# An attention kernel followed by two MoE layers: gammas' product on GpSimd, twelve constant products ahead of the first q and k, and the first MoE's weight conversions placed beside attention pairs

## The chip, the cores and the metric

One Trainium2 chip, one core. A NeuronCore has TensorE (matmuls, into PSUM), VectorE, ScalarE, GpSimd and SyncE, which run separate in-order instruction queues, and 16 DMA engines. In the profile they are PE (with PEld for its weight loads), DVE, ACT, POOL and SP; in this kernel SP's queue issues nearly all DMAs. The metric is the device time in microseconds of one execution; lower is better.

## The reference

```python
def attn(q, k, v, g_q, g_k):          # batch 4, heads 12, seq 448, head_dim 64
    q_n, k_n = rmsnorm(q, g_q), rmsnorm(k, g_k)
    scores = q_n @ k_n.T / sqrt(64)
    p = softmax(scores)               # max subtracted, sum + 1e-9
    return p @ v                      # v is 0.1 * randn

def moe(x, w_in, w_out, g_ln):        # 1792 tokens, 768 -> 1024 -> 768
    h = x @ w_in
    solu = h * softmax(h)
    ln = (solu - mean) / sqrt(var + 1e-6) * g_ln
    return ln @ w_out

def moe2(x, w_in, w_out):             # 768 -> 2048 -> 768
    h = x @ w_in
    return (h - tanh(h)) @ w_out

out = moe2(moe(attn(...) as 1792 tokens x 768, ...), ...)
```

The weights of both MoE layers arrive as float64, so their DRAM tensors are read as pairs of int32.

## The kernel before

**Attention.** The 48 heads are worked on as 24 pairs p. `load_qk` (L209) loads q and k of a pair, `norm` (L241) computes the reciprocal root mean squares (square on ScalarE, reduction and the rest on VectorE) and scales, `qk_trans` (L264) transposes on TensorE, splits each value into a high and a low float32r part, multiplies k by `gam` (the product of both gammas and the scale, one [128, 1] column) and for p > 0 spreads the parts by DMA into the layouts `Q` and `K`. `maxima` (L325) gets each row's maximum from one matmul and a VectorE reduction; `spread` (L345) transposes the maxima and puts them by a small DMA (`q<-nt`) into a row of `Q`, so that the scores of `weights` (L357) come out with the maximum subtracted; ScalarE takes the exponential. `pv` (L391) multiplies by v, `pv_fin` and `x_norm` divide by the sum, and x_norm stores the pair's result into the DRAM tensor `xd` (L432), which tells in the trace when a pair is done.

**First MoE.** Tokens are worked on in four blocks of 384, 384, 384 and 640. `x_split` (L490) loads a block of xd, `moe_h` (L500) is the first product, `layer_norm` (L539) the activation, `moe_lnT` (L571) transposes and `moe_x2` (L585) is the second product. `stage(b)` (L602) does x_split(b), moe_lnT(b-1), moe_h(b), layer_norm(b) and moe_x2(b-1).

**Weights.** `Stream` (L96) brings weight tiles in: `fetch` (L111) loads 512 KB of raw int32 pairs by SP's queue into the pool `raw_p` (two buffers), and `convert` (L117) makes a high and a low float32r part of it (512 KB together). A converted tile that is needed in later blocks too is saved to DRAM (L164) and loaded again from there (L174). There are twelve input tiles ("in") and twelve output tiles ("out", multiplied by the layer norm's gamma on the way). For a saved tile the conversion is: ScalarE's absolute value (L135), VectorE's maximum (L136), shift (L140) and two merges (L144, L147); then for an input tile ScalarE's copy (L160) and GpSimd's subtraction (L161), for an output tile four ScalarE copies (L154) and four VectorE operations (L155). `conv(n)` (L167) brings the stream up to item n and looks two items ahead with its loads. In the kernel before, input tiles come by conv in `moe_h(0)`, and the twelve output tiles are converted in `moe_h(1)` (L534 to 536), three after each quarter of the input weights, in the pool Bp["w"] of five buffers that also holds the reloaded input tiles.

**Order.** The list `attn` holds every attention step with a slot and a step in it (`at`, L438): slot 2p begins pair p's maxima, its norm is at slot 2p - 3, its last step at slot 2p + 3. `attn_next` runs the next (slot, step). The program first runs all steps up to slot 15 (L679), then `overlap(b, batch)` (L682) spreads the remaining ones over stages 0, 1 and 2 (slots 16 to 27, 28 to 39, 40 and up). The written order isn't the queues' order: the tile framework plans with a simulated timeline, so that an instruction whose operands and buffers are there early in the plan may be queued ahead of earlier-written ones. So the raw loads and conversions of the first input tiles, written in stage 0, stand in the queues among the first attention pairs. After attention, the second MoE (`h2`, `out2`, from L786 on) runs in eight rounds over its own weight stream.

The start: identity and constants are built, the two gammas are loaded by ScalarE's DMA queue (L676) and multiplied on VectorE (L678):

```python
nc.vector.scalar_tensor_tensor(out=gam, in0=gam, scalar=scale, in1=gam2, op0=ALU.mult, op1=ALU.mult)
while attn_left(H + 3):
    attn_next()
```

## Time and profile before

| | |
|---|---|
| median of 3 runs | 1116.38 us (1116.32 to 1119.02) |
| profiled execution, its own time | 1117.29 us |
| its span on the core | 1115.4 us |
| PE busy | 1045.5 us, 94% |
| DVE busy | 694.8 us, 62% |
| ACT busy | 493.8 us, 44% |
| POOL busy | 234.2 us, 21% |
| moved by DMA | 171.20 MB |

Busy times are those of the one profiled execution; matmuls are pipelined, so a busy PE isn't one at its peak. A row of a timeline gives the start, the duration, the engine, the line of the kernel, the operation with output and inputs, how many of them, and in brackets how long the engine was idle before and what ended that. DMA share is the mean busy share of the 16 DMA engines; the clock column is the TensorE clock that the throttle granted, as a fraction.

### The profile page before, as it was taken

What the parts mean: (1) busy time and instruction counts of PE and PEld (TensorE: products, weight loads), DVE (VectorE), ACT (ScalarE), POOL (GpSimd) and SP (SyncE); (2) the same over time, 40 slices, a digit from 0 to 9 for tenths busy, and PEclk for the clock granted to TensorE, in tenths of its full rate; (3) what the DMA queues carried; (4) which work ended last, traced back from release to release, by engine and by line L of the source; (5) the groups of instructions that cost most, each with busy time, mean ns of one, the idle gap of its engine ahead of it and who ended that gap; (6) DMA issues with size and microseconds to landing.
All of it is one profiled execution on the core that took longest, in us unless ns stands there. A gap on an engine that the chain in (4) does not pass through costs nothing.

```text
span 1115.4 us, 15528 instructions
## 1 busy us (share of the span) xinstructions
PE 1045.5 (94%) x5528; PEld 874.9 (78%) x5528; DVE 694.8 (62%) x1313; ACT 493.8 (44%) x1004; POOL 234.2 (21%) x204
## 2 busy tenths in 40 slices
PE   4989999988987899998999999999999999999998
PEld 2555666657774778777899989898999989898987
DVE  8776687788797353724655057375767666675444
ACT  4677777777676454744246154321212121212110
POOL 2411123131102000001500025242314241322000
PEclk9999999999998999998999999999999999999999
DMA  7987779957997978655767443121111111120004
GB/s 184 258 230 192 184 213 282 229 167 209 288 285 231 307 207 260 182 174 174 249 205 242 156 152 92 34 65 49 57 38 57 58 58 57 57 57 1 1 29 170
DMA packets 108945, 171.20 MB, mean 153 GB/s; under 512 B 31748, under 2 KB 73156, under 8 KB 108868
## 3 DMA queue, kind: packets, MB, share of 16 engines
q1 hardware_dynamic: 107568, 170.20, 52.2%
q8 instruction: 44, 0.72, 0.3%
q14 instruction: 33, 0.27, 0.1%
q10 hardware_dynamic: 1300, 0.01, 0.1%
HBM read 109.32 MB, written 29.10 MB: 124 GB/s over the span
## 4 chain that ended last, share of the span: by engine, by line
PE 74%; DMA 12%; DVE 7%; ACT 5%; issue 2%; SPq 1%; POOL 0%; ACTq 0%; DVEq 0%; POOLq 0%
PE pvps L401 8%; PE ops L183 7%; PE ops L184 7%; PE ops L182 7%; PE h2ps L183 7%; PE h2ps L184 7%; PE h2ps L182 7%; PE sps L378 4%; PE x2ps L182 3%; PE x2ps L183 3%; PE x2ps L184 3%; PE hps L182 2%; PE hps L184 2%; DMA xr<-xd 2%; PE hps L183 2%; DMA q<-wq 2%
## 5 line engine op out<-in xcount | busy, mean ns | idle before, releaser
L780 DVE TENSOR_TENSOR ob<-ops,ob 128x384 f32<-128x384 f32 x196 | 108.6, 555 | 103.0 <-PE ops L184 102.4
L161 POOL TENSOR_TENSOR w<-val,w 128x512 fp32r<-128x512 f32 x60 | 81.3, 1356 | 419.7 <-ACT w L160 402.6
L401 PE MATMUL pvps<-pf,va 128*128 128x448 f32 (+1 forms) x384 | 160.9, 583 | 1.7 <-ACT pf L387 1.7
L183 PE MATMUL ops<-w,gT 128*128 128x384 f32 x448 | 150.7, 336 | 0.0
L182 PE MATMUL ops<-w,gT 128*128 128x384 f32 x448 | 150.6, 336 | 0.0
L184 PE MATMUL ops<-w,gT 128*128 128x384 f32 x448 | 150.5, 336 | 0.0
L343 DVE TENSOR_REDUCE nm<-mps 128x1 f32<-128x448 f32 x168 | 102.9, 620 | 66.3 <-PE mps L342 57.6
L183 PE MATMUL h2ps<-x2s,w 128*128 128x512 f32 (+1 forms) x384 | 141.0, 367 | 0.0
L184 PE MATMUL h2ps<-x2s,w 128*128 128x512 f32 (+1 forms) x384 | 140.9, 367 | 0.0
L182 PE MATMUL h2ps<-x2s,w 128*128 128x512 f32 (+1 forms) x384 | 140.6, 367 | 0.0
L378 PE MATMUL sps<-q,k 128*128 128x448 f32 (+1 forms) x368 | 117.5, 413 | 20.7 <-ACT pf L387 9.2
L757 ACT ACTIVATE th<-h2ps 128x512 f32<-128x512 f32 (+1 forms) x64 | 34.8, 544 | 181.2 <-PE h2ps L184 180.9
L378 PEld LDWEIGHTS sps<-q,k 128*128 128x128 f32 (+1 forms) x368 | 63.0, 186 | 55.5 <-ACT pf L387 17.8
L387 ACT ACTIVATE pf<-sps 128x448 f32<-128x448 f32 x167 | 88.3, 539 | 37.9 <-PE sps L378 29.5
L182 PE MATMUL hps<-w,xs 128*128 128x256 f32 x336 | 101.0, 301 | 2.7 <-DMA w<-w_in 2.5
L184 PE MATMUL hps<-w,xs 128*128 128x256 f32 x336 | 96.5, 288 | 0.0
L183 PE MATMUL hps<-w,xs 128*128 128x256 f32 x336 | 95.6, 285 | 0.0
L401 PEld LDWEIGHTS pvps<-pf,va 128*128 128x128 f32 (+1 forms) x384 | 61.6, 195 | 42.1 <-issue 34.3
L342 PE MATMUL mps<-k,q 128*128 128x448 f32 (+1 forms) x144 | 77.2, 545 | 14.9 <-DVE nm L343 5.6
L258 POOL TENSOR_TENSOR qn<-qk,rr 112x512 f32<-112x512 f32 x44 | 47.5, 1101 | 192.5 <-DVE rr L239 88.9
L183 PEld LDWEIGHTS ops<-w,gT 128*128 128x128 f32 x448 | 84.3, 188 | 4.6
L182 PEld LDWEIGHTS ops<-w,gT 128*128 128x128 f32 x448 | 84.2, 188 | 4.6 <-DVE ob L780 0.2
(117 smaller groups left out, 2091.7 us busy)
## 6 DMA issues: line engine op xcount, KB each, us to landing
w<-w_out SPq DMA_DIRECT2D x48, 512.0 KB
raw<-in_moe_w_in_dram SPq DMA_DIRECT2D x36, 512.0 KB
raw<-in_moe_w_out_dram SPq DMA_DIRECT2D x36, 512.0 KB
w<-w_in SPq DMA_DIRECT2D x36, 512.0 KB
k<-wk SPq DMA_DIRECT2D x46, 224.0 KB
q<-wq SPq DMA_DIRECT2D x46, 224.0 KB
w_in<-w SPq DMA_DIRECT2D x12, 512.0 KB
w_out<-w SPq DMA_DIRECT2D x12, 512.0 KB
```

What stands on the lines that cost most here:

```text
L161: nc.gpsimd.tensor_tensor(out=w[:, 1], in0=x, in1=w[:, 0].bitcast(F32), op=ALU.subtract)
L182: nc.tensor.matmul(ps, lhsT=a[0], rhs=w[0], start=first, stop=False)
L183: nc.tensor.matmul(ps, lhsT=a[0], rhs=w[1], start=False, stop=False)
L184: nc.tensor.matmul(ps, lhsT=a[1], rhs=w[0], start=False, stop=last)
L258: eng.tensor_tensor(out=qn[:, a].rearrange("p c h d -> p h c d"), in0=t[:, a], in1=rr[:, a].rearrange("p h (c o) -> p h c o", o=1).to_broa ...
L342: nc.tensor.matmul(ps, lhsT=qh[:, f:f + 128], rhs=kh, start=True, stop=True)
L343: nc.vector.tensor_reduce(out=nm_t[p][:, c:c + 1], in_=ps, axis=AX.X, op=ALU.max, negate=True)
L378: nc.tensor.matmul(o, lhsT=K[p % NQ][:, i, z, k0:k0 + m], rhs=qcols(Q[p % NQ], slice(0, 128), p, i, z), start=(z == 0), stop=(z == 1))
L387: nc.scalar.activation(out=x, in_=ps, func=AF.Exp)
L401: nc.tensor.matmul(pv_t[n], lhsT=w, rhs=pc_t.pop((n, j))[r], start=first, stop=last)
L757: nc.scalar.activation(out=th, in_=ps, func=AF.Tanh)
L780: nc.vector.tensor_tensor(out=o, in0=ps, in1=o, op=ALU.add)
```

## The change

Four edits. The product of the gammas moves to GpSimd, as two instructions. Twelve matmuls of the identity with itself, into a PSUM tile that nobody reads, are issued after the first load. The input tiles 0 to 4 of the first MoE are converted at attention slots 3, 5, 7, 9 and 11, each raw load written directly ahead of its conversion, with no look ahead. The twelve output tiles are no longer converted in moe_h(1): `conv_out` fetches and converts them at slots 4, 6, 8, 10, 12 and 13 to 19, in a new pool "wp" with one raw buffer and one result buffer. Up to the end of the steps before stage 0, raw loads are pinned: they stand on SP's queue behind all DMAs written ahead of them.

```diff
+    pinned = [True]
...
-        def fetch(self, kind, i):
+        def fetch(self, kind, i, pool=None):
             if (kind, i) not in self.raw:
                 src, (a, b) = source(kind, i)
-                t = self.raw[kind, i] = raw_p.tile([128, a, b, 2], I32, tag="raw", name="raw64")
-                nc.sync.dma_start(out=t, in_=src)
+                t = self.raw[kind, i] = (pool or raw_p).tile([128, a, b, 2], I32, tag="raw", name="raw64")
+                dma = nc.sync.dma_start(out=t, in_=src)
+                if pinned[0]:
+                    tc.keep_in_program_order(dma)
...
-        def conv(self, n):
+        def conv(self, n, ahead=2):
...
-                self.load(self.nc + 2)
+                self.load(self.nc + ahead)
...
+    def conv_out(i):
+        ws.fetch("out", i, A["wp"])
+        ws.convert("out", i, A["wp"], True)
+
...
+    for i in range(5):
+        at(3 + 2 * i, 3, lambda i: ws.conv(i + 1, 0), i)
+    for i in range(12):
+        at((4, 6, 8, 10, 12, 13, 14, 15, 16, 17, 18, 19)[i], 3, conv_out, i)
...
                         ws.conv(w0 + 3 * qq + 6)
-                        if b == 1:
-                            for i in range(3 * qq, 3 * qq + 3):
-                                ws.convert("out", i, Bp["w"], True)
...
-        ("pc", 6), ("xu", 1), ("xo", 1), ("small", 2),
+        ("pc", 6), ("wp", 1), ("xu", 1), ("xo", 1), ("small", 2),
...
     attn_next()
+
+    warm = ps_x.tile([128, 4, CP], F32, tag="x", name="warm")
+    for _ in range(12):
+        nc.tensor.matmul(warm.rearrange("p c q -> p (c q)")[:, 0:128], lhsT=idf, rhs=idf, start=True, stop=True)
...
-    nc.vector.scalar_tensor_tensor(out=gam, in0=gam, scalar=scale, in1=gam2, op0=ALU.mult, op1=ALU.mult)
+    nc.gpsimd.tensor_scalar(out=gam, in0=gam, scalar1=scale, scalar2=None, op0=ALU.mult)
+    nc.gpsimd.tensor_tensor(out=gam, in0=gam, in1=gam2, op=ALU.mult)
     while attn_left(H + 3):
         attn_next()
+    pinned[0] = False
```

## Rows read from the trace of the kernel before

**Rows 1.** The page's busy times: engine, busy us, share of the span, instructions.

```profile
PE 1045.5 (94%) x5528; PEld 874.9 (78%) x5528; DVE 694.8 (62%) x1313; ACT 493.8 (44%) x1004; POOL 234.2 (21%) x204
```

**Rows 2.** Windows: stretch, length, busy PE, PEld, DVE, ACT, POOL; clock, DMA share, GB/s.

```profile
15.00:60.60 45.60, 40.44 (x117) 22.42 (x117) 36.08 (x71) 27.57 (x59) 15.28 (x14) 1.00 0.94 253
60.60:142.20 81.60, 75.33 (x315) 47.04 (x315) 53.86 (x106) 60.59 (x131) 14.74 (x18) 0.98 0.76 194
...
142.20:237.40 95.20, 86.90 (x442) 61.25 (x440) 75.37 (x140) 69.33 (x147) 25.66 (x24) 0.98 0.89 238
237.40:394.60 157.20, 134.22 (x679) 102.02 (x680) 117.30 (x260) 103.06 (x234) 22.91 (x26) 0.96 0.85 256
394.60:508.00 113.40, 111.70 (x617) 89.86 (x616) 49.64 (x98) 63.05 (x130) 5.84 (x9) 1.00 0.71 205
280.00:320.00 40.00, 35.92 (x206) 28.14 (x204) 33.06 (x74) 29.85 (x75) 5.75 (x6) 0.96 1.02 293
```

**Rows 3.** Timeline of the start, all engines.

```profile
5.33 0.63 ACT L250 ACTIVATE sq<-qk 112x512 f32<-112x512 f32 x1 [1.10 <-DMA qk<-in_q_dram]
8.14 0.16 DVE L678 SCALAR_TENSOR_TENSOR gam<-gam,gam 128x1 f32<-128x1 f32 x1 [3.18 <-DMA gam<-in_g_k_dram]
8.21 1.27 DVE L252 TENSOR_REDUCE ss<-sq 112x8 f32<-112x512 f32 x2
...
11.01 0.98 PE L268 MATMUL qkps<-idf,qn 112*128 112x112 f32 x4 [11.01 <-DVE nr L238]
...
12.03 0.63 ACT L279 ACTIVATE k<-qkps,gam 128x448 fp32r<-128x448 f32 x1 [0.15 <-PE qkps L268]
```

**Rows 4.** Timeline of TensorE around 41 us, then windows as in Rows 2.

```profile
40.58 0.57 PE L373 MATMUL sps<-q,k 64*128 64x448 f32 x1
42.68 0.37 PE L373 MATMUL sps<-q,k 64*128 64x448 f32 x1
12.00:16.00 4.00, 2.25 (x9) 1.61 (x9) 3.95 (x15) 3.00 (x9) 0.00 (x0) 1.00 0.83 239
60.00:64.00 4.00, 1.62 (x7) 1.08 (x8) 2.46 (x4) 1.56 (x5) 0.00 (x0) 1.00 0.97 253
64.00:68.00 4.00, 4.00 (x14) 1.84 (x13) 2.97 (x8) 3.21 (x9) 0.00 (x0) 0.65 0.80 236
```

**Rows 5.** Timeline of SP's queue: raw weight loads and stored pairs.

```profile
10.68 0.65 SPq L115 DMA_DIRECT2D raw<-in_moe_w_in_dram  x1
...
60.59 0.58 SPq L432 DMA_DIRECT2D xd<-xo  x1
...
68.49 0.43 SPq L115 DMA_DIRECT2D raw<-in_moe_w_in_dram  x1
...
142.24 0.54 SPq L432 DMA_DIRECT2D xd<-xo  x1
...
179.71 0.40 SPq L115 DMA_DIRECT2D raw<-in_moe_w_out_dram  x1
```

**Rows 6.** Lines by form: conversions from 20 to 60 (first row), from 260 to 360.

```profile
L161 POOL TENSOR_TENSOR w<-val,w 128x512 fp32r<-128x512 f32 x5 | 7.1, 1427 | 23.0 <-DVE nr L237 17.1 <-ACT w L160 5.9
...
L154 ACT ACTIVATE w<-val,gln 128x128 fp32r<-128x128 f32 x48 | 15.3, 390 | 0.9 <-DVE val L147 0.8
L155 DVE SCALAR_TENSOR_TENSOR w<-val,gln,w 128x128 fp32r<-128x128 f32 x48 | 14.3, 348 | 0.5 <-DMA va<-in_v_dram 0.2 <-ACT w L154 0.2
L144 DVE SCALAR_TENSOR_TENSOR val<-raw,val 128x512 int32<-128x512 int32 x11 | 8.8, 797 | 0.2
L147 DVE SCALAR_TENSOR_TENSOR val<-raw,val 128x512 int32<-128x512 int32 x10 | 7.5, 749 | 0.1
L135 ACT ACTIVATE val<-raw 128x512 f32<-128x512 f32 x10 | 6.7, 669 | 8.1 <-DMA raw<-in_moe_w_out_dram 6.4 <-DVE nm L343 1.4
L140 DVE TENSOR_SCALAR val<-val 128x512 int32<-128x512 int32 x11 | 5.4, 488 | 0.1
```

**Rows 7.** Timeline of ScalarE: the longest early wait for a raw load.

```profile
28.78 0.67 ACT L135 ACTIVATE val<-raw 128x512 f32<-128x512 f32 x1 [2.37 <-DMA raw<-in_moe_w_in_dram]
```

**Rows 8.** GpSimd's one small operation, line L563: min/median/max ns.

```profile
L563 POOL TENSOR_TENSOR rs<-rs,mhalf x14: 544/560/2137, 229.6 to 592.5; 128x1 f32<-128x1 f32 x14
```

## The prediction, made before the changed kernel was run

> **What bounds the kernel now.** I read the busy times first, then the windows stage by stage, then the timeline of the start, then the SP queue. Over the whole span TensorE is busy 94% [rows 1], which says little: the 600 us after the attention, more than half of it, are not touched by the change. The stages ahead of them differ, and the windows [rows 2] show it. There the attention of four batches runs with the first MoE; I name the stretches *front* (15 to 60.6, until the first pair's result is stored), *prologue* (60.6 to 142.2, six further pairs, almost only attention), *stage 0* (to 237.4), *stage 1* (to 394.6) and *stage 2* (to 508). The reader is to compare the last two. Both do 384 tokens of the first MoE's two products beside about six pairs of attention; stage 1 issues 679 matmuls in 157.2 us, stage 2 617 in 113.4. Stage 2 is TensorE-bound (111.7 of 113.4 busy), while in stage 1 VectorE is busy 117.3 against 49.6, ScalarE 103.1 against 63.1, and the DMA share is 0.85 against 0.71. What stage 1 has and stage 2 has not is the conversion of the twelve tiles of output weights. The prologue has nearly no conversions and runs at 13.6 us a pair; the front has five complete ones of input weights [rows 6], nine raw loads being issued from 10.68 to 68.49 [rows 5], and a DMA share of 0.94.
>
> **The change part by part.**
>
> *Gammas' product on GpSimd.* VectorE sits 3.18 us for gamma's DMA at 8.14, with the first norm's reduction queued behind it; ScalarE's squares are over by 5.96 [rows 3]. Off that queue, the reduction starts about 5, then waits at most for ScalarE, and the first transposes move from 11.01 to about 8.0: 3.0 us. The product is first used at 12.03, so then at 9.0. It is now two instructions; the only small GpSimd instruction in the trace takes 560 ns [rows 8], so gamma is ready near 8.1 + 2 x 0.56 = 9.2, and the gain is 2.7. Behind it on GpSimd stand zero fills not needed for several us. Bounds 2 to 3.
>
> *Twelve constant products.* They need the identity only and fill TensorE from some 3 us to the first transposes, on an idle engine: nothing lost. What they can give is the clock. The granted-clock column says 1.00 from the start, but the durations do not: the same matmul takes 0.57 at 40.58 and 0.37 at 42.68 [rows 4], so TensorE works at 1.2 GHz until 41 us and at 2.4 from there. Later the clock falls once after a stretch with 1.62 of 4 us busy (granted 0.65 next) [rows 4]. From 12 to 16 TensorE is busy 2.25 of 4 at the low level, which is some 1.1 of 4 at the high one: thinner than the stretch after which it fell. So I think it likelier that the raised clock is lost again before the dense part. The Trainium skill, "TensorE: Matmul & The Clock Gate", Part 1, says that the default state is throttled, that activity releases it and that idleness takes it back; by its release alone the products would pay in full, by its second half they would not. The fall at 64 agrees with the second half, the rise at 41 with the first.
>
> *The front.* Its DMA work is 0.94 x 45.6 = 42.9 us. Seven of the nine raw loads and five saves lie in it; 512 KB at 293 GB/s per 1.02 share [rows 2] is 1.8 us each, so half of that work leaves. At the prologue's pace (81.6 us / 315 matmuls = 0.26) the front's 117 matmuls are 30.3 us, 15 less than now: with the 2.7 that is -18 if the clock is high from the beginning. If it is low until 41 as before, only the some 60 matmuls after that gain (19.6 to 15.6): -7. Without raw loads in the way TensorE becomes dense earlier and its clock should rise earlier; I take **-13**.
>
> *The prologue* pays. Input tiles 0 to 4 are converted at slots 3 to 11 and output tiles at slots 4 to 15, so 13 conversions with 13 raw loads and 13 saves lie in these 12 slots, which held two raw loads. DMA: 0.76 x 81.6 = 62.0, less 2 x 1.8, plus 13 x 3.4 (3.65 by the mixed rate above; the attention part of that mix moves at 194/0.76 = 255 GB/s by its own row, so the conversions' part is faster) = 102.6; at the 1.02 that 280 to 320 holds [rows 2] it is 100.6 us. VectorE: an output tile costs 4 x 0.348 + 0.797 + 0.749 + 2 x 0.488 = 3.9, an input tile 2.5 [rows 6]: 53.9 + 5 x 2.5 + 8 x 3.9 = 97.6. ScalarE: 0.67 + 4 x 0.39 = 2.2 and 1.3: 60.6 + 6.5 + 17.8 = 85. The DMA queues end last: 100.6 instead of 81.6, **+19**. Bounds: +5, if the conversions slide into later slots (their pool has one raw buffer and one result buffer, so one conversion must free the raw buffer before the next load, and nothing in the attention waits for them); +28, if ScalarE also waits for each raw load.
>
> *Stage 0* keeps its seven input tiles and gets four output tiles: 13.6 us of DMA, 15.6 of VectorE. It loses raw loads of output weights that were issued there early, the first at 179.71 [rows 5]. Its DMA work is 0.89 x 95.2 = 84.7, its VectorE 75.4: there is room for most. **+6**, bounds 0 and +13.
>
> *Stage 1* gives back. At stage 2's pace it takes 113.4 plus the 62 further matmuls at 134.22/679 = 0.20 each, 12.3: 125.7 instead of 157.2, **-32**. It also does norms and loads of six pairs where stage 2, at the end of attention, does fewer; so -20 to -35. What is late next in stage 1 is TensorE itself. Nothing waits for the saved output tiles there before its second product.
>
> *Order on the SP queue.* Pinned raw loads cost issue time in any place (some 0.4 each [rows 5]); moved behind the attention's loads they no longer delay those of the first pairs. The pin itself adds no wait: a pinned load may be issued later than written, not earlier. Each new load or save that stands at the head of SP and waits delays the small loads of maxima behind it; that is in the +28.
>
> Sum: -13 + 19 + 6 - 32 = **-20** on a span of 1115.4. The profiled execution took 1117.29, the median is 1116.38: **1096**.
>
> **The rivals.**
>
> *A, slack absorbs it.* The clock stays high (-18), conversions slide to where engines have room (+5, +3), stage 1 reaches stage 2's pace with less overhead (-35): -45, 1071. For: TensorE's peak demand in the prologue is below its span, and at 280 to 320 VectorE is busy 33.06 of 40 under a full DMA while TensorE still holds 35.92 [rows 2]. Against: DMA demand of prologue and stage 0 together (62 + 84.7 + 17 x 3.4 less the early raw loads, about 195) exceeds their 176.8 us.
>
> *B, the price is conserved.* The twelve output tiles cost 31.5 us in stage 1, 2.6 each. At that price prologue and stage 0 pay 31 for them, and the five input tiles take with them what they cost in the front: 0, within 3 us of 1116. The change would move the load, not hide it. The same time results if the planner's order lets the output tiles slide so far that stage 1 still holds them.
>
> *C, slower: ScalarE waits for the raw loads.* Now a raw load is issued long ahead; even so ScalarE waited 2.37 us at the head of its queue for one [rows 7]. After the change the load is issued just ahead of its conversion, and behind the waiting instruction on ScalarE stand the exponentials for which TensorE waits. 13 x 2.4 = 31 on top of 85 busy is 116, +35 in the prologue; four more in stage 0, +13; front only -10, stage 1 -28: +10, 1126. It decides from about 1.6 us a conversion upward, where ScalarE's 85 + 13 x 1.6 = 106 passes the DMA's 100.6 and adds to its jitter.
>
> **How the numbers follow.** Forecast 0.5, A 0.2, B 0.13, C 0.17. A measurement of this kernel can tell about 0.3% (3.3 us) from no change. The forecast's own bounds reach from 1077 to 1112, all on the faster side. Faster: 0.5 + 0.2 + a quarter of B = 0.73; same: 0.10; slower: C = 0.17. The range runs from 1071 (A) to 1115 (most of B); it leaves out C and the ends of A.
>
> **What would show it.** First transposes at 8.0 to 8.5; matmul durations of the first maxima at the low level again after some us; the first pair stored at 47 to 50 and the seventh at 142 to 150; a DMA share near 1.0 between them; no output conversion after the start of stage 1, and stage 1 at 122 to 137 us with VectorE below half. Wrong would be: a share well below 1 in the prologue with ScalarE waiting on raw loads (C), conversions in stage 1 (B), or a full clock through the front (A). The second MoE should only shift.

## The result, and the profile after

| | before | after |
|---|---|---|
| median | 1118.67 us (6 runs, 1116.32 to 1123.95) | 1135.36 us (6 runs, 1128.35 to 1141.29) |
| profiled execution, span | 1117.29, 1115.4 us | 1135.99, 1134.2 us |

The changed kernel is slower: ratio 1.0148, 95% interval 1.0101 to 1.0195. The forecast was 1096.0, range 1071 to 1115. (The lines of the code that the trace names have moved down by 4 to 14: L135 is now L139, L279 is L283, L342 is L346, L378 is L382.)

The busy times of the changed kernel's page answer to [rows 1]. TensorE is busy 15 us longer for the same work and 24 extra matmul records (the constant products, 4.5 us ahead of the first transposes); VectorE's, ScalarE's and the DMA's totals have not moved. So nothing else was added but time in which TensorE waits or runs slowly.

```profile
PE 1060.5 (94%) x5552; PEld 883.4 (78%) x5552; DVE 694.4 (61%) x1312; ACT 493.5 (44%) x1004; POOL 237.0 (21%) x206
```

The windows of the changed kernel, cut at the same events as [rows 2] (first and seventh pair stored, then the starts of stage 1 and stage 2); the columns are those of [rows 2]:

```profile
15.00:63.40 48.40, 45.07 (x116) 25.22 (x116) 25.57 (x52) 22.68 (x49) 9.78 (x10) 0.60 0.55 139
63.40:168.60 105.20, 85.88 (x339) 51.95 (x338) 79.74 (x170) 77.53 (x176) 22.47 (x22) 0.94 0.92 254
168.60:288.70 120.10, 96.99 (x436) 62.28 (x435) 106.23 (x212) 84.80 (x186) 32.91 (x30) 0.93 0.86 254
288.70:414.00 125.30, 121.72 (x671) 97.57 (x670) 69.43 (x143) 77.26 (x165) 17.25 (x21) 0.99 0.78 217
```

| stretch | before | after | difference | forecast |
|---|---|---|---|---|
| front, to the first pair's store | 45.6 (to 60.6) | 48.4 (to 63.4) | +2.8 | -13 (-7 to -18) |
| prologue | 81.6 | 105.2 | +23.6 | +19 (+5 to +28) |
| stage 0 | 95.2 | 120.1 | +24.9 | +6 (0 to +13) |
| stage 1 | 157.2 | 125.3 | -31.9 | -32 (-20 to -35) |
| rest of the span | | | -0.6 | 0 |

The sum is +18.8, the span's difference. Stage 1 gave back exactly what was forecast; the front gave nothing, and stage 0 cost four times its term. A part of the prologue's time is work taken ahead: it holds 339 matmul records against 315 before, 15 of the 24 more of the first MoE's first product.

**The start.** The timeline of the changed kernel answers to [rows 3]:

```profile
3.09 4.51 PE L676 MATMUL warm<-idf 128*128 128x128 f32 x24 [3.09 <-POOL idf masks.py:199]
7.93 0.19 POOL L693 TENSOR_TENSOR gam<-gam,gam 128x1 f32<-128x1 f32 x1 [1.02 <-DMA gam<-in_g_k_dram]
7.96 0.60 PE L272 MATMUL qkps<-idf,qn 112*128 112x112 f32 x4 [0.36 <-DVE qn L262]
15.86 1.06 ACT L254 ACTIVATE sq<-qk 112x1024 f32<-112x1024 f32 x1 [4.22 <-DMA qk<-in_q_dram]
16.83 0.62 ACT L283 ACTIVATE k<-qkps,gam 128x448 fp32r<-128x448 f32 x1
17.50 0.74 PE L338 MATMUL mps<-k,qd 128*128 128x448 f32 x1 [5.68 <-ACT k L283]
```

The first transposes start at 7.96 as forecast (8.0), at the high clock (0.60 instead of 0.98 for four). But k's copy on ScalarE, which is ready to run then, stands behind the square of pair 2 (L254), and that waits 4.22 us for its DMA. So the first maxima start at 17.50, while the kernel before has 15.44 and three us less would have been 12.4. TensorE has nothing from 11.8 to 17.5 and its clock falls. The windows of four us show that it stays down (PE busy, then the clock column):

```profile
12.00:16.00 4.00, 0.00 (x0) 0.00 (x0) 0.29 (x1) 0.14 (x1) 0.00 (x0) 0.65 0.88 225
28.00:32.00 4.00, 4.00 (x9) 1.99 (x7) 0.86 (x3) 0.54 (x1) 2.04 (x2) 0.50 0.99 246
48.00:52.00 4.00, 4.00 (x8) 1.64 (x7) 2.07 (x6) 0.85 (x3) 0.61 (x1) 0.50 0.01 3
52.00:56.00 4.00, 4.00 (x9) 1.55 (x7) 1.35 (x3) 2.01 (x4) 2.15 (x3) 0.73 0.28 59
```

**The prologue.** In all of it ScalarE waits 9.9 us in 5 for raw loads; the longest of these waits shows the chain. All engines of the changed kernel, timeline from 82 us, rows picked: a raw load of an output tile is issued at 82.74, ScalarE's absolute value (L139) stands at the head of its queue 4.39 us for it, VectorE's maximum (L140) waits 4.68 us for that, a reduction of maxima (L347) stands behind VectorE's conversion steps, and TensorE's next maxima matmul (L346) waits 3.36 us for the reduction.

```profile
82.74 0.44 SPq L117 DMA_DIRECT2D raw<-in_moe_w_out_dram  x1
...
88.17 1.22 ACT L139 ACTIVATE val<-raw 128x512 f32<-128x512 f32 x2 [4.39 <-DMA raw<-in_moe_w_out_dram]
88.86 0.43 DVE L140 TENSOR_SCALAR val<-val 128x512 f32<-128x512 f32 x1 [4.68 <-ACT val L139]
...
90.00 0.62 DVE L347 TENSOR_REDUCE nm<-mps 128x1 f32<-128x448 f32 x1
...
90.67 1.02 PE L346 MATMUL mps<-k,q 128*128 128x448 f32 x2 [3.36 <-DVE nm L347]
```

And the windows around it: ScalarE did nothing at all and VectorE 0.18 us from 84 to 88, TensorE 1.24 us of the next four; and then four us at 0.61 of the clock.

```profile
84.00:88.00 4.00, 3.32 (x15) 1.92 (x13) 0.18 (x1) 0.00 (x0) 1.91 (x3) 1.00 0.90 272
88.00:92.00 4.00, 1.24 (x3) 0.67 (x4) 3.10 (x7) 3.75 (x8) 0.00 (x0) 0.97 1.09 238
92.00:96.00 4.00, 3.89 (x13) 1.85 (x11) 4.00 (x8) 3.36 (x9) 0.00 (x0) 0.61 0.92 204
```

**Stage 0.** VectorE is busy 106.23 of 120.1 us here. The forecast had 75.4 + 15.6 = 91. The groups by line of this stretch (168.6 to 288.7) show what more there is: twelve conversions of saved tiles (L140) where the forecast had eleven, and two of tiles that aren't saved (L142), which belong to the second MoE. The lines of the conversions are 46.3 us of VectorE here against 21.1 before, so 25 of the 31 us that it has more. In the kernel before, those two have their raw loads at 343.96 and 355.17, in stage 1; in the changed kernel SP issues them from 248.96 on, two together: with the output tiles gone from stage 1 the raw buffers are free early.

```profile
L140 DVE TENSOR_SCALAR val<-val 128x512 f32<-128x512 f32 x12 | 5.7, 476 | 7.4 <-ACT val L139 7.4
...
L142 POOL TENSOR_SCALAR val<-raw 128x512 f32<-128x512 f32 x2 | 3.7, 1855 | 8.5 <-DMA raw<-in_moe_w_in_dram 8.5
```

They meet block 0's layer norm. Two of the windows of that stretch:

```profile
268.00:272.00 4.00, 1.64 (x3) 0.58 (x3) 4.00 (x9) 1.10 (x2) 0.00 (x0) 0.65 1.00 240
272.00:276.00 4.00, 1.85 (x3) 0.79 (x4) 4.00 (x9) 1.23 (x3) 0.00 (x0) 0.50 1.00 356
```

From 264 to 284 TensorE is busy 12.1 of 20 us (2.63 + 1.64 + 1.85 + 3.28 + 2.71 in the five windows), the last 12 of them at half clock, and its waits from 262 on name VectorE's reductions of maxima (5.1 us in 3).

### The profile page after: what moved, and what is told of

It is laid out like the page before. It is cut to its first block, busy times and chain, and to the rows that moved or that the text cites. A ratio compares the mean times of both kernels' runs of the same rounds, so it can differ in the third digit from the quotient of the medians.

```text
span 1134.2 us, 15575 instructions
## 1 busy us (share of the span) xinstructions
PE 1060.5 (94%) x5552; PEld 883.4 (78%) x5552; DVE 694.4 (61%) x1312; ACT 493.5 (44%) x1004; POOL 237.0 (21%) x206
## 4 chain that ended last, share of the span: by engine, by line
PE 71%; DMA 15%; DVE 7%; ACT 4%; issue 2%; SPq 1%; POOL 0%; ACTq 0%; DVEq 0%; POOLq 0%
PE pvps L405 7%; PE h2ps L187 7%; PE ops L187 7%; PE h2ps L188 7%; PE ops L188 7%; PE ops L186 7%; PE h2ps L186 7%; DMA w<-w_in 3%; PE sps L382 3%; PE x2ps L186 3%; PE x2ps L188 3%; PE x2ps L187 3%; PE hps L186 2%; PE hps L187 2%; PE hps L188 2%
## 5 line engine op out<-in xcount | busy, mean ns | idle before, releaser
L796 DVE TENSOR_TENSOR ob<-ops,ob 128x384 f32<-128x384 f32 x196 | 108.5, 554 | 104.0 <-PE ops L188 103.5
L405 PE MATMUL pvps<-pf,va 128*128 128x448 f32 (+1 forms) x384 | 164.9, 592 | 5.1 <-ACT pf L391 4.7
L165 POOL TENSOR_TENSOR w<-val,w 128x512 fp32r<-128x512 f32 x60 | 81.6, 1361 | 407.3 <-ACT w L164 406.0
L347 DVE TENSOR_REDUCE nm<-mps 128x1 f32<-128x448 f32 x168 | 102.4, 617 | 92.6 <-PE mps L346 74.6
L382 PE MATMUL sps<-q,k 128*128 128x448 f32 (+1 forms) x368 | 123.8, 431 | 24.9 <-DMA q<-nt 9.3
L382 PEld LDWEIGHTS sps<-q,k 128*128 128x128 f32 (+1 forms) x368 | 64.7, 190 | 62.9 <-DVE nm L347 15.9
L405 PEld LDWEIGHTS pvps<-pf,va 128*128 128x128 f32 (+1 forms) x384 | 62.7, 199 | 46.6 <-issue 35.0
L142 POOL TENSOR_SCALAR val<-raw 128x512 f32<-128x512 f32 x48 | 80.1, 1670 | 33.2 <-DMA raw<-in_moe_w_in_dram 16.9
L346 PE MATMUL mps<-k,q 128*128 128x448 f32 (+1 forms) x144 | 73.4, 520 | 14.4 <-ACT pf L391 6.9
```

The lines of the kernel that those rows point to most:

```text
L142: nc.gpsimd.tensor_scalar(out=fv, in0=fh, scalar1=2.0 ** -15, scalar2=None, op0=ALU.max)
L165: nc.gpsimd.tensor_tensor(out=w[:, 1], in0=x, in1=w[:, 0].bitcast(F32), op=ALU.subtract)
L346: nc.tensor.matmul(ps, lhsT=qh[:, f:f + 128], rhs=kh, start=True, stop=True)
L347: nc.vector.tensor_reduce(out=nm_t[p][:, c:c + 1], in_=ps, axis=AX.X, op=ALU.max, negate=True)
L382: nc.tensor.matmul(o, lhsT=K[p % NQ][:, i, z, k0:k0 + m], rhs=qcols(Q[p % NQ], slice(0, 128), p, i, z), start=(z == 0), stop=(z == 1))
L405: nc.tensor.matmul(pv_t[n], lhsT=w, rhs=pc_t.pop((n, j))[r], start=first, stop=last)
```

## The experiments

Sixteen kernels. Ratios are to the kernel before, run beside each on the same chip; between rows it is the ratios that can be compared. Each profile is of one execution.

| run | what it is | median us | ratio, 95% interval |
|---|---|---|---|
| e1 | before, gammas' product moved | 1117.9 | 1.0019 [0.9990, 1.0047] |
| e2 | before, twelve products added | 1119.7 | 1.0000 [0.9965, 1.0036] |
| e3 | before, all conversions moved | 1126.9 | 1.0109 [1.0062, 1.0157] |
| e4 | after, k's copy ahead | 1131.5 | 1.0137 [1.0101, 1.0174] |
| e5 | e4 without the products | 1137.7 | 1.0142 [1.0076, 1.0209] |
| e6 | e3, less VectorE work | 1132.4 | 1.0111 [1.0040, 1.0181] |
| e7 | e3, fewer DMAs | 1128.0 | 1.0083 [1.0045, 1.0122] |
| e8 | before, input tiles moved, pinned | 1134.1 | 1.0107 [1.0047, 1.0168] |
| e9 | e3, input tiles at slots -2 to 2, free | 1131.0 | 1.0122 [1.0077, 1.0167] |
| e10 | after, nothing pinned | 1122.1 | 1.0043 [1.0011, 1.0074] |
| e11 | before, without the output tiles | 1087.7 | 0.9722 [0.9681, 0.9762] |
| e12 | e8, without the output tiles | 1106.7 | 0.9895 [0.9858, 0.9931] |
| e13 | e3, nothing pinned | 1121.2 | 1.0025 [1.0001, 1.0049] |
| e14 | e3, only output loads pinned | 1136.7 | 1.0165 [1.0128, 1.0203] |
| e15 | e8, not pinned | 1118.6 | 0.9999 [0.9974, 1.0024] |
| e16 | e8, looking two tiles ahead | 1126.8 | 1.0071 [1.0044, 1.0098] |

### One part at a time: e1, e2, e3

**e1**, the gammas' product alone:

```diff
-    nc.vector.scalar_tensor_tensor(out=gam, in0=gam, scalar=scale, in1=gam2, op0=ALU.mult, op1=ALU.mult)
+    nc.gpsimd.tensor_scalar(out=gam, in0=gam, scalar1=scale, scalar2=None, op0=ALU.mult)
+    nc.gpsimd.tensor_tensor(out=gam, in0=gam, in1=gam2, op=ALU.mult)
```

> The kernel before with the gammas' product on GpSimd and nothing else. Queue theory (the product's new place makes the planner queue k's first copy on ScalarE behind an instruction that waits for a DMA, which costs more than the 3 us that VectorE wins): first transposes near 8, but the first maxima not before 15, first pair stored at 60 or later, time 1117 to 1123. Rival (the move by itself is the small gain that was forecast, and the late k copy in the changed kernel comes from the conversions' new order): first maxima near 12.5, 1113 to 1116.

Measured 1.0019: nothing. The timeline shows why the 2.9 us won at the transposes (8.14) aren't there at the first maxima (16.27, against 15.44 before):

```profile
8.14 0.98 PE L268 MATMUL qkps<-idf,qn 112*128 112x112 f32 x4 [8.14 <-DVE nr L238]
...
15.04 0.66 ACT L135 ACTIVATE val<-raw 128x512 f32<-128x512 f32 x1 [2.90 <-DMA raw<-in_moe_w_in_dram]
15.60 0.63 ACT L279 ACTIVATE k<-qkps,gam 128x448 fp32r<-128x448 f32 x1
...
16.27 0.74 PE L334 MATMUL mps<-k,qd 128*128 128x448 f32 x1 [3.97 <-ACT k L279]
```

Here it is the first conversion's absolute value that is queued ahead of k's copy and waits for its raw load; in the changed kernel it is pair 2's square. The wait removed from VectorE's queue is replaced by one in ScalarE's.

**e2**, the twelve products alone (the four added lines of the diff).

> The kernel before with the twelve constant products and nothing else. Lost-clock theory: the products raise the clock, the thin stretch up to 20 us loses it, and the dense part starts low and rises again near 40 or later; first pair stored at 58 to 66, time 1115 to 1123. Rival (the clock holds): scores before 30 us last 0.37 instead of 0.57, first pair stored before 54, time 1106 to 1112.

Measured 1.0000. The windows show the clock up early, down at the thin place (0.69 of 4 us busy from 8 to 12), and then at the low level until 56, though TensorE is busy 4.00 of 4 in the windows at 28, 48 and 52:

```profile
12.00:16.00 4.00, 1.96 (x6) 1.23 (x7) 3.62 (x14) 2.53 (x9) 0.00 (x0) 0.50 0.80 245
...
52.00:56.00 4.00, 4.00 (x7) 1.44 (x6) 1.31 (x2) 0.64 (x1) 0.50 (x1) 0.50 0.37 96
56.00:60.00 4.00, 3.58 (x13) 2.10 (x13) 2.10 (x5) 3.86 (x7) 0.47 (x1) 0.98 0.98 238
```

In the kernel before, durations fall to the high level's at 42.68 [rows 4]. The first pair is stored at 68.6 in this profile instead of 60.6, the seventh at 147.8 instead of 142.2, and the span is 1121.7 instead of 1115.4: in this execution most of the late start stays to the end. Over all runs the ratio is 1.0000 with an interval of 0.36% to either side, so a price of some 4 us can be neither shown nor excluded.

**e3**, the conversions alone (the change without those two edits).

> The kernel before with the conversions moved and pinned and the other two parts left out. Conserved-price theory: the prologue and stage 0 are together 45 to 50 us longer, stage 1 32 shorter, and the front gains some 5 because the raw loads left it: 1122 to 1130. Rival (the loss is the start's, the conversions pay for themselves): 1105 to 1116.

Measured 1.0109: the loss is in the conversions. The first pair is stored at 54.3 us (60.6 before), the seventh at 160.0 (142.2), the thirteenth at 291.6 (258.7), the nineteenth at 421.9 (411.7): 6 us won in the front, 24 lost in the prologue, 15 more up to the thirteenth pair, and 23 won back in stage 1. The changed kernel's 1.0148 against 1.0109 leaves 0.4% for the other two edits; the intervals overlap, and without the pin (e10 against e13, below) they add 0.2%.

### The start again: e4, e5

**e4**, the changed kernel with the squares of pairs 2 and 3 kept in written order, so that k's copy comes first:

```diff
-            nc.scalar.activation(out=sq[:, a], in_=t[:, a], func=AF.Square)
+            sqi = nc.scalar.activation(out=sq[:, a], in_=t[:, a], func=AF.Square)
+            if p in (2, 3):
+                tc.keep_in_program_order(sqi)
```

> The changed kernel whole, but the squares of pairs 2 and 3 on ScalarE may not be queued ahead of what is written before them, so that k's first copy does not stand behind a square that waits for its DMA. Queue theory: the first maxima begin near 12 instead of 17.5, TensorE's idle 5.7 us goes, the clock rises by 35 instead of 54, the first pair is stored by 50, and the time falls by 10 to 15 to 1120 to 1126. Rival (the low clock of the front comes from the products' early rise and fall in any case): the start moves by 5 and the time by less than 6, to 1129 to 1134.

k's copy now runs at 11.80 and the first maxima at 12.49, five us earlier than in the changed kernel; TensorE is busy 3.39 of the four us from 12 to 16. Still the clock is lost (0.57). The windows of half a us place the fall at the very start of this stretch, so the dense work came too late to show whether it would have kept the clock; in the four us ahead (8 to 12) TensorE was busy 1.81. The clock is back only at 48 to 52:

```profile
12.49 0.67 PE L340 MATMUL mps<-k,qd 128*128 128x448 f32 x1 [0.54 <-ACT k L285]
```

```profile
12.00:12.50 0.50, 0.01 (x1) 0.01 (x1) 0.45 (x2) 0.50 (x2) 0.00 (x0) 1.00 1.01 329
12.50:13.00 0.50, 0.50 (x1) 0.20 (x1) 0.50 (x1) 0.46 (x1) 0.00 (x0) 0.59 1.10 355
12.00:16.00 4.00, 3.39 (x6) 1.57 (x6) 3.95 (x8) 0.96 (x2) 0.00 (x0) 0.57 0.96 264
...
48.00:52.00 4.00, 4.00 (x9) 1.53 (x9) 1.80 (x3) 1.33 (x3) 2.44 (x3) 0.73 0.00 0
```

So the queue position is confirmed as the cause of the late maxima, but not as the cause of the loss: 1.0137 against 1.0148. The time, 1131.5, is in the rival's 1129 to 1134.

**e5** is e4 without the four lines of the products.

> The kernel of e4 (changed kernel, k's first copy not behind the squares of pairs 2 and 3) without the twelve constant products. Products theory (a clock raised early and lost comes back later than one that was never raised: 54, 56 and 50 us with the products, 41, 32 and 35 without): first maxima near 12.5, full clock by 28 to 36, first pair stored at 45 to 50, 4 to 10 us less than the conversions alone: 1117 to 1123. Rival (the late rise has nothing to do with the products): full clock again near 50, first pair at 56 to 60, 1127 to 1132.

1137.7 instead of the 1117 to 1123 expected: missed. The first pair is stored at 59.0 and the seventh at 171.2. It should have been e3 with an earlier start. Two pinned squares move the first raw load of an input tile to 54.2 and thereby all the conversions; what of the time that explains wasn't settled. But on the products the profile speaks for the rival. The same maxima matmul takes 0.74 at 40.37 and 0.37 at 52.04, so the clock is back at about 50, as in e4 with the products, and the first pair is stored in the rival's 56 to 60:

```profile
40.37 0.74 PE L348 MATMUL mps<-k,q 128*128 128x448 f32 x1
...
52.04 0.37 PE L348 MATMUL mps<-k,q 128*128 128x448 f32 x1
```

So the late return of the clock isn't shown to come from the products.

### What in the conversions: e6, e7

**e6** is e3 with three of VectorE's four assembly steps left out for output tiles (their maximum, shift and first merge):

```diff
-                nc.vector.tensor_scalar(out=fv, in0=fv, scalar1=2.0 ** -15, scalar2=None, op0=ALU.max)
+                if kind != "out":
+                    nc.vector.tensor_scalar(out=fv, in0=fv, scalar1=2.0 ** -15, scalar2=None, op0=ALU.max)
...
+            if kind != "out":
```

> The kernel of e3 (conversions alone), and for the output tiles three of VectorE's four steps that assemble the value are left out (the maximum, the shift, the first merge), 1.8 us a tile, 21 us in all; DMAs and ScalarE as they were. VectorE theory (the moved tiles are paid on VectorE, behind whose steps the maxima wait): 10 to 16 us less than e3, 1111 to 1117. DMA theory (paid on the DMA queues): 0 to 4 less, 1123 to 1127.

**e7** is e3 with the raw pairs of one output tile loaded once and used for all twelve, and one result saved (22 transfers of 512 KB left out):

```diff
-        ws.fetch("out", i, A["wp"])
+        if i == 0:
+            ws.fetch("out", 0, A["wp"])
+            one_raw.append(ws.raw["out", 0])
+        ws.raw["out", i] = one_raw[0]
...
+            if save and kind == "out" and i > 0:
+                saved[kind, i] = saved[kind, 0]
```

> The kernel of e3 (conversions alone), but raw output weights are loaded once and the converted tile is saved once, the other eleven conversions working on the same raw tile: 22 transfers of 512 KB, some 39 us of DMA, are left out, and so is the wait of one load for the raw buffer; VectorE's and ScalarE's work is as it was. DMA theory: 15 to 30 us less than e3, 1097 to 1112, the seventh pair stored 10 or more earlier. VectorE theory: 0 to 6 less, 1121 to 1127.

Neither is faster than e3 beyond the intervals: 1.0111 and 1.0083 against 1.0109; e6's 1132.4 and e7's 1128.0 lie above both of their expectations. The prologues (between first and seventh store) of e3, e6 and e7:

```profile
54.30:160.00 105.70, 85.67 (x339) 51.88 (x338) 80.37 (x171) 78.22 (x177) 22.93 (x22) 0.94 0.93 257
```

```profile
62.20:174.80 112.60, 89.24 (x336) 51.24 (x335) 76.91 (x160) 81.53 (x184) 21.11 (x22) 0.94 0.94 250
```

```profile
54.30:158.30 104.00, 82.23 (x317) 46.62 (x315) 91.91 (x189) 80.06 (x183) 22.11 (x22) 0.97 0.75 206
```

With the DMA share down from 0.93 to 0.75 the prologue is 104.0 instead of 105.7 us: the DMA queues did not set its end, although the forecast that they would gave nearly the right length. Still the transfers held the conversions back: without them ScalarE starts 14 conversions in e7's row against 11 in e3's, and VectorE is busy 91.91 us instead of 80.37. Nor did VectorE's amount of work set the end (the second row, 13 conversions); there the comparison is weaker, as e6's clock came back between 52 and 56 us instead of 35 and its first pair 8 us later.

### Where the price lies: e8, e11, e12, e9, e10

**e8** moves only the five input tiles (slots 3 to 11, loads pinned); the output tiles are converted in `moe_h(1)` as before:

```diff
+    for i in range(5):
+        at(3 + 2 * i, 3, lambda i: ws.conv(i + 1, 0), i)
```

> The kernel of e3 with the output tiles converted in the first product of the second block as before: of the change only the five input tiles at pinned places stay. Conserved-price theory: the front gains 6, the prologue pays 6 to 10 for the five tiles, the rest as before: 1115 to 1122. Rival (the input tiles are the part that pays, since the front had no room and the prologue has): 1106 to 1112.

**e11** is the kernel before with the twelve output conversions left out (the second product takes the input tiles in their place), **e12** is e8 with the same left out:

```diff
-                        if b == 1:
-                            for i in range(3 * qq, 3 * qq + 3):
-                                ws.convert("out", i, Bp["w"], True)
```

> The kernel before with the twelve output conversions left out (raw load, arithmetic, save); the second product reloads the saved input tiles in their place, so that every reload is there. It prices the twelve conversions where they were: by the comparison of stages 1 and 2, 32 us, so 1083 to 1089; by pairs (pairs 12 to 18 against the changed kernel's, 21 us), 1095 to 1099.

> The kernel of e8 (five input tiles at pinned slots 3 to 11) with the output conversions left out as in e11. Input-tile theory: the moved input tiles cost the same 12 to 16 us here, so 1096 to 1103 if e11 is at 1086, and e3 less this run is the price of the twelve output tiles beside pairs 2 to 9, again some 26 to 30. Rival (the loss of the input tiles comes from crowding with other conversions later on): within 5 us of e11.

The twelve output tiles cost 1118.3 - 1087.7 = 30.6 us where they were; the forecast's comparison of stages 1 and 2 gave 31.5. The five input tiles cost 12 us by the ratio or 15 by the medians (e8 against before), and 19.0 in e12 against e11, at slots 3 to 11, where the forecast had them as a gain in the front and 5 x 3.4 us of transfers in the prologue. Both came out slower than expected, e8 (1134.1) than its theory and its rival. **e9** puts them at slots -2 to 2, not pinned, with the output tiles' loads pinned:

```diff
-        at(3 + 2 * i, 3, lambda i: ws.conv(i + 1, 0), i)
+        at((-2, -1, 0, 1, 2)[i], 3, lambda i: ws.conv(i + 1, 0), i)
```

> The kernel of e3 (conversions alone) with the five input tiles at slots -2 to 2 and their raw loads not pinned, so that they are loaded and converted in the front as in the kernel before; the output tiles stay pinned beside pairs 2 to 9. Input-tile theory (the whole loss is that the front gave away five conversions that cost it little, and the prologue pays 2.8 us for each): the first pair stored near 60, 8 to 14 us less than e3, 1113 to 1120, no more than 0.3% from the kernel before, since the output tiles cost beside pairs 2 to 9 what they cost in stage 1. Rival (the output tiles lose too): 1123 to 1128.

1.0122: missed, the expectation was 1113 to 1120. **e10** is the changed kernel with `pinned = [False]`:

> The changed kernel with the raw loads not pinned and nothing else changed. Input-tile theory: raw loads and the first input tiles float back into the front, and the time falls to 1116 to 1126. Rival (the place of the conversions is set by their slots, and the pin only orders loads): 1131 to 1137.

1.0043 against 1.0148: leaving out the pin, the only edit, wins back about 1.05%, 12 us, most of the loss. It moves more than the order on SP's queue, though: the raw loads of the output tiles now start at 12.89 instead of 64.29 and end at 164.95 instead of 207.86, and the conversions go with them.

### The pin: e13 to e16

**e13** is e3 with `pinned = [False]`; **e14** is e3 with `if pinned[0] and kind == "out":`; **e15** is e8 with `pinned = [False]`; **e16** is e8 with `ws.conv(i + 1, 2)`, so that the next two raw loads stand directly behind each conversion.

> The kernel before with the moved conversions alone (no product of the gammas on GpSimd, no constant products), and the raw loads not pinned: SP may issue them as early as a buffer is free. Theory, the pin is what makes the moved tiles dear: the changed kernel without its pin took 1122.1, the moved conversions with the pin 1126.9 against 1135.4 for the whole change; if the two gains add, this one takes 1113 to 1116, no slower than before (1118). Rival, the conversions cost the same wherever they stand beside attention: 1124 to 1128, as with the pin. A ratio below 0.997 would make it the first version faster than before.

> As the run without a pin, but the raw loads of the twelve output tiles stay pinned; those of the five input tiles (slots 3 to 11) are free. Theory, it is the five pinned input tiles that cost 16 to 19 us: the time is that of the run without any pin, 1113 to 1116. Rival, the output tiles' loads at the head of the SP queue cost as much: 1124 to 1128, as with all loads pinned.

> The five input tiles at slots 3 to 11, not pinned; the output tiles in stage 1, as before. With the pin this took 1134.1, against 1118 before. Theory, the pin carries the cost: 1116 to 1122, because the loads can again be issued early. Rival, the later place in the list carries it whether pinned or not: 1130 to 1136. ScalarE's waits for the raw loads from 15 to 290 us (10.6 us in 5 with the pin) and TensorE's waits for the row of maxima (14.7 us in 8 with the pin, 5.2 in 3 before) should fall with the time, whichever of them carries the cost.

> The five input tiles at slots 3 to 11, pinned, but each conversion followed by the pinned raw loads of the two next input tiles (look ahead of two, as in the stream of before), so that a load stands two slots, some 14 us, ahead of its conversion. Theory, the cost is ScalarE waiting at the head of its queue for a load that was issued just ahead (3.4 us at most, 2.1 on average): these waits vanish and the time falls from 1134 to 1118 to 1124. Rival, the cost is not that wait but the work of the conversions beside the attention's pairs 2 to 6, or the loads' place on the SP queue in front of the small loads of the maxima: 1130 to 1137.

e15 equals the kernel before (0.9999): unpinned, the planner puts the input tiles' loads back where they had been, from 8.55 to 65.63 us (before 10.68 to 68.49 [rows 5]), whatever their written slot. Pinned, in e8, they run from 31.04 to 134.69. The windows of e15 and then of e8, 15 to 60 and 60 to 160 us:

```profile
15.00:60.00 45.00, 38.79 (x116) 21.32 (x115) 39.64 (x72) 27.90 (x58) 15.52 (x14) 0.92 0.93 253
60.00:160.00 100.00, 93.35 (x416) 61.39 (x414) 67.39 (x126) 71.92 (x155) 21.43 (x24) 0.97 0.79 197
```

```profile
15.00:60.00 45.00, 42.50 (x119) 24.30 (x117) 25.34 (x52) 22.14 (x47) 10.45 (x10) 1.00 0.61 148
60.00:160.00 100.00, 84.21 (x345) 52.35 (x345) 66.65 (x130) 70.31 (x151) 21.20 (x23) 0.95 0.82 218
```

Up to 60 us the conversions that e8 doesn't have yet take 14 us of VectorE and a third of the DMA share in e15, and taking them away lets TensorE issue only 119 matmuls instead of 116. That is not because they cost nothing there: e8's TensorE is busy 42.50 of 45, at the low clock until about 48 us. In e3, whose matmuls are the same up to 35 us but whose clock rose then, it issued 130 by 60 us:

```profile
15.00:60.00 45.00, 39.92 (x130) 22.41 (x128) 27.83 (x57) 24.71 (x55) 8.94 (x10) 0.99 0.71 181
```

After 60 us the same conversions take 71 matmuls from TensorE in 100 us. As the place of the conversions changes with the pin here, the pair gives the price of the later place, not of a load just ahead of its reader. The waits of e8 and e15, 15 to 290 us: in e8 TensorE waits for the small load of maxima (`q<-nt`) 14.7 us in 8 instead of 6.9 in 4, VectorE's conversions for ScalarE's 11.6 instead of 6.2. ScalarE's own waits for raw loads are not longer in e8 (12.9 us in 6 in all, 14.4 in 7 in e15). With the look ahead of e16 TensorE's waits for maxima fall to 5.0 in 4, ScalarE still waits 11.3 us for raw loads of input tiles (10.6 in e8), and the ratio is 1.0071 against e8's 1.0107, with overlapping intervals and between its two expectations. The look ahead did not give the lead that was expected (14 us): the absolute values of moved tiles that waited started 6 to 8 us after their loads were issued, at 62.7 for a load of 55.52 and at 80.5 for one of 73.91. So e16 is no test of a long lead.

For the output tiles e13 and e14 differ by one edit, the pin, and by 15.5 us; e13 lies between its two expectations, e14 above both. Waits of ScalarE, VectorE and TensorE from 15 to 290 us (total, times, longest); e13:

```profile
ACT val L139 <- DMA raw<-in_moe_w_out_dram: 9.6, 8, 2.2
DVE val L140 <- ACT val L139: 6.8, 8, 2.3
PE mps L346 <- DVE nm L347: 7.7, 12, 1.6
```

and e14:

```profile
ACT val L139 <- DMA raw<-in_moe_w_out_dram: 24.3, 10, 5.0
DVE val L140 <- ACT val L139: 28.0, 12, 5.1
PE mps L346 <- DVE nm L347: 17.0, 12, 5.3
```

The chain is the one of the episode at 82 us above: raw load, ScalarE, VectorE, maxima, TensorE; all three links grow. But the waits are not all that the pin changes. In the changed kernel ScalarE's are hardly longer than in e10, which differs by the pin (18.8 us in 9, 17.1 in 8 from 15 to 290 us), and in e13 too a raw load is issued only 5 to 6 us ahead of the absolute value that waits for it (31.16 and 37.2, 50.25 and 55.5), as in e14 (137.24 and 142.7, 151.39 and 156.9). What differs in both pairs is when the work is done. The seventh pair is stored at the same time with and without the pin (168.6 in the changed kernel, 168.9 in e10; 167.0 in e14, 169.8 in e13), but by then ScalarE has started 12 and 11 of the 24 conversions with it and 18 without. What is left is paid behind: from there to the nineteenth pair's store the changed kernel takes 260.3 us and e10 246.9, e14 267.1 and e13 250.8. How much of the pin's price is the waits and how much the later place no run separates.

Without any pin (e13) the moved output tiles cost 1121.2 - 1087.7 = 33.5 us, against 30.6 in stage 1 (by the ratios 3.0% and 2.8%): about the same price beside the first pairs, so even the best form of the move gains nothing.

## Why the prediction was wrong, step by step

**Sign wrong, two terms of the sum wrong, one reason missing.** The terms were -13, +19, +6, -32; measured +2.8, +23.6, +24.9, -31.9.

*Gammas and products.* The transposes came at 7.96, as worked out (8.0). Gamma was ready at 8.1; I had priced a small GpSimd instruction at the 560 ns of [rows 8], and the two took 0.24 and 0.19. The step that failed is "the gain is 2.7": it took k's copy to follow as soon as its operands are there, and did not ask what stands ahead of it in ScalarE's queue. Pair 2's square stood there (in e1 a conversion). That the clock would be raised early and lost again before the dense part was right; that it would then be low until after 52, instead of 41, was in none of the cases. The rule of the Trainium skill that the prediction cites ("TensorE: Matmul & The Clock Gate", Part 1: activity releases the clock, idleness takes it back) agrees with the fall; the low level from 28 to 52, with TensorE busy 4.00 of every 4 us, is not what its first half leads one to expect.

*The front, -13: wrong by 16.* The failed step is that TensorE's "clock should rise earlier". TensorE did become dense without the raw loads (busy 45.07 of 48.4), but at the low clock until after 52. With the conversions out of the front, the first pair's store goes with the rise of the clock: 53.9 to 54.3 in e12, e7 and e3, where it rises at 34 to 35 us, 58.5 to 59.5 in e4, e5 and e8 (47 to 51), 62.2 and 63.4 in e6 and the changed kernel (52 to 56). So taking the conversions away did help, by 6.3 us at the best (e3), the -7 end of my bounds; "at the prologue's pace the front's 117 matmuls are 30.3 us" promised more than any run gave (39.3 in e3). Which of these fronts a kernel gets I could not have read from its instructions: e3 and e8 have the same ones up to 35 us.

*The prologue, +19: 23.6, in its bounds, but by luck, not by its reason.* I let the DMA queues end last at 100.6 us. e7 took a fifth of their load away and the prologue was 104.0 instead of 105.7. TensorE's waits in the changed prologue are for ScalarE's exponentials (9.4 us), the small loads of maxima (5.9) and VectorE's reductions (3.7); the first and the last stand behind conversions in their engines' queues, and ScalarE's 9.9 us for raw loads, which I had kept in the upper bound of 28, are a part of what delays them. The stretch also held 11 conversions instead of 13, and 24 matmul records more than before.

*Stage 0, +6: +24.9, outside its bounds.* The term was mis-sized, and the trace names how: VectorE had 106 us of work instead of 91, with one saved conversion that slid in from the prologue and two conversions of the second MoE that came from stage 1. I had listed only the loads that leave stage 0. It is the question that should have been asked of "room for most": what will the planner put there.

*Stage 1, -32: -31.9.* Right, and for its reason: stage 2 as its twin. TensorE is busy 121.72 of 125.3, VectorE's 117.3 fell to 69.43, and e11 gives the tiles' price as 30.6.

*Order on the SP queue: "the pin itself adds no wait" is the sentence that cost the sign.* The reasoning was that a pinned load can be issued later than written, not earlier, and so does no harm to others. What it missed is that without the pin the loads and conversions run far ahead of their written slots: by the seventh pair's store 18 conversions have started in e10, 12 in the changed kernel. Later they stand beside more work, and ScalarE's and VectorE's in-order queues hold the exponentials and the maxima behind them. e10 against the changed kernel, e14 against e13, and e8 against e15 give 12, 15 and 12 to 15 us for the pin with all that it moves.

*The bounds.* Added up, the four terms' own bounds run from -48 to +14, 1068 to 1130. The "1077 to 1112, all on the faster side" is narrower than that, without a reason given; by the bounds themselves a slower kernel was not left to C alone.

*The rivals.* A (slack absorbs) fell with the front. B (price conserved) is what the runs without a pin show: 33.5 us against 30.6 for the output tiles, and 1.0025 in all. C (ScalarE waits for the raw loads) had the sign, with 1126 nearest to 1135, and named a mechanism that is there. Its size came out differently: in the prologue ScalarE waited 9.9 us for 11 conversions, 0.9 each and below the 1.6 from which I had it decide. I had counted only ScalarE's own time: the wait goes on to VectorE (13.4 us in the prologue, in 5) and from its queue to the maxima, for whose reductions TensorE waits 17.7 us in 17 from 15 to 290 us, against 10.9 in 16 in e10 and 9.1 in 14 in the kernel before. At 0.17 it had too small a chance; the row of ScalarE waiting 2.37 us even for a load issued long ahead [rows 7] should have weighed more than the pin's "no wait".

**Open.** That the pin costs 12 to 15 us is shown; that it does so by the chain of waits is argued, since it also moves the conversions. The prices don't add up. Pinned input tiles cost 12 to 19 us by themselves and pinned output loads 15, yet both together (e3) cost 0.84%, 9 us, more than neither (e13); e3 is faster than e14, which pins less. e5 and e6 were slower than expected with no wait that I could name; their late clock in the front (about 50 us, and between 52 and 56, against 35 in e3) is a part of it in their profiles. The prologue of e5 and e6 (112 and 113 us) is 7 us longer than e3's, and stretches at a low clock come and go: of the 58 four-us windows from 60 to 292 us, 4 are below 0.9 of the clock in the kernel before, 10 in the changed one, 15 in e3, 8 in e8, 8 in e15. (Ahead of 60 us the column can't be used for all of them, see the last section.) As e15 is as fast as before with 8, and e8 over 1% slower with 8, the clock doesn't order these runs. What the late clock of the front costs by the end wasn't measured, with one profiled execution of each kernel. That the small loads of maxima come late in e8 because of the raw loads' place on the SP queue was not tried separately. No version beat the kernel before.

## What to carry to other kernels

A high DMA share is not yet a bound: take the transfers away in an experiment before giving them a price (here the share fell from 0.93 to 0.75 and the prologue by 1.7 us). When two starts are compared, compare them at the same clock, and read it from durations of the same matmul: two kernels with the same instructions up to 35 us had fronts 5 us apart. Pinning loads to their written place takes away what the planner had won by running them ahead, and with them their readers, so ask where the work stood before and what it will stand beside. And when work leaves a stage, ask what the planner will draw into the room, and what stands ahead of the instruction that you made ready earlier.

## What the runs showed of the hardware

TensorE's clock in the front was the surprise. In the three runs with the twelve products and their profile shown here (after, e2, e4) the granted clock is high at the first transposes (four in 0.60 us instead of 0.98) and lost between 11.5 and 13.5 us, after windows in which TensorE was busy 1.77 (after), 0.69 (e2) and 1.81 (e4) of the four us from 8 to 12. It is back only at 50 to 56 us, with TensorE busy 4.00 of 4 us in the low windows shown from 28 us on.

The products are not shown to be the reason. Without them the same dense work rose to the high level at 41 us in the kernel before [rows 4], and in e3 at about 35:

```profile
32.00:36.00 4.00, 4.00 (x9) 2.23 (x9) 1.25 (x2) 0.46 (x2) 0.00 (x0) 1.00 0.82 230
36.00:40.00 4.00, 4.00 (x18) 2.33 (x16) 1.58 (x3) 2.55 (x6) 0.00 (x0) 1.00 0.00 1
```

But in e8, whose matmuls are e3's, in the same order and with the same durations (within 0.01 us), up to 35 us, it rose only at about 48, and in e5 (above) at about 50, both without the products:

```profile
36.00:40.00 4.00, 4.00 (x9) 1.95 (x9) 0.62 (x1) 0.72 (x2) 0.00 (x0) 1.00 0.00 1
43.09 0.74 PE L346 MATMUL mps<-k,q 128*128 128x448 f32 x1
...
53.12 0.36 PE L346 MATMUL mps<-k,q 128*128 128x448 f32 x1
```

And e10, with the products, had it back between 32 and 36 us. So the same matmuls can wait for the high level 13 us longer in one execution (e8) than in another (e3), and what decides it was not found.

The two rows of e3 show also that the clock column reads 1.00 on both sides of the rise, while TensorE, busy throughout, goes from 9 matmuls in four us to 18; in e8 it reads 1.00 at the low level. Ahead of the first change of level that it records the column can't be trusted, durations can.
